# A new order for the first stage of a fused attention and two-layer feed-forward kernel: 128-token pieces of all heads, and two weight loads moved ahead

## The chip, the cores and the metric

The kernel runs on one core of a Trainium2 chip. The metric is the device time of one execution in microseconds (us), the median over the runs. A core has a matrix engine (TensorE, PE in the rows, with PEld for its weight loads), a vector engine (VectorE, DVE), a scalar engine (ScalarE, ACT), a general engine (GpSimd, POOL), and a sync engine (SyncE, SP) that issues most transfers. Each engine works through its own queue in order.

## The reference

Inputs are q, k, v of shape (4 batches, 8 heads, 576 tokens, 64), and five weight matrices which arrive as 64-bit floats.

```python
q_d, k_d, v_d = means over 4 neighbouring tokens            # 144 rows a head
out_up = repeat(softmax(q_d @ k_d.T / 8) @ v_d, 4)          # long range
s = where(abs(i - j) < 4, q @ k.T / 8, -1e9)                # a band of 7 tokens
out_local = softmax(s) @ v
x = (out_up + out_local) as 2304 tokens x 512
x = (silu(x @ w_gate) * (x @ w_val)) @ w_out                # 512 -> 1536 -> 512
h = x @ w2_in                                               # 512 -> 2048
return (h * clip(h + 3, 0, 6) / 6) @ w2_out                 # 2304 x 512
```

## The kernel before, in words

The 2304 tokens go through the feed-forward layers in five blocks (`BLOCKS`, 512 or 384 tokens). A block is 68 units in a fixed order, each with one 128-wide slice of a weight matrix: pairs of `G` (gate), `V` (value), `O` (out), then `H` and `P` of the second layer. A `G`, `V`, or `H` unit is twelve products of 128x128 by 128x512 (`products`, L390): fp32 is split into a high part and a remainder, and three of the four products are taken. The first four of the twelve pairs need only the high part of x.

In block 0 each unit's weights come from the input as a raw piece of 512 KB (`load_raw`), are decoded by `decode_a` (ScalarE, tile `top`) and `decode_b` (VectorE, tile `w`), and split by `split_hi` (ScalarE) and `split_lo` (VectorE) into tile `wr`. Four raw buffers exist at first, so raw piece n+4 is loaded only after `decode_b` of piece n. From unit 0 on, `prefetch` decodes piece i+5 and i+4 and splits pair i+3 while unit i runs. The decoded weights are written to `kept` for the later blocks.

Before unit 0, `first_batch` does the attention of batch 0 on its own (the later batches' attention lies beside the feed-forward work). This stage is called the front. All its PE, DVE and ACT instructions stand in an order written out by hand, `FRONT`, which fixes each of the three queues (`Ordered` keeps program order). A step's name is its function and its index:

- `T`, `E`, `R`: transpose a piece of q or k on PE, evacuate it to SBUF, and sum over groups of four tokens on DVE.
- `dS dM dE dT dP dO dN` (index: pair of heads, 0 to 3): the long-range attention: scores (PE), maximum (DVE), exponential (ACT), transpose (PE), copy (ACT), times v (PE), normalize into `odN` (DVE).
- `SC M W N PT Pa Pd V` (index: 96-token tile, 0 to 5): the local attention: scores and band (PE), maximum (DVE), exponential (ACT, tile `held`), normalize (DVE), transpose (PE), copies (ACT and DVE, tile `turned`), times v (PE, tile `fO`). `V` also adds the long-range part: matmuls of `odN` with `fours`, which repeats each row four times.
- `Xh`, `Xl` (`Yh`, `Yl` for the columns of block 1): write x as high part (ACT) and remainder (DVE) to tile `xr`.
- `to`, `de`, `hi`, `lo`: `decode_a`, `decode_b`, `split_hi`, `split_lo` of the first raw pieces; `de(i)` also issues the load of raw piece i+4.
- `two`, `sums`: GpSimd gathers token sums of batch 1 by transfers and adds; `two` starts behind `M3`.

In the kernel before a `T` is a pair of heads and half of the tokens (three transposes of 96 tokens), and `dS(c)` needs the pieces of pair c alone, while `SC` needs all pairs. `dS` and `PT` use the PSUM banks `acc2` and `acc3`; `dT`, `dO`, `V` use `pa` and `px`; `SC` uses `acc0`, `acc1` or the two `mm` banks. `fill` issues bf16 matmuls whose result nobody reads; `FILL_T`, `FILL_S`, `FILL_P`, `FILL_END` place 69 of them, and `WARM` puts 14 larger ones at the very start.

The SP queue issues, in this order: 16 loads of q and k by head (L148), four loads of v for the long-range values (`load_vd`, tiles `spread` and `vd`), four raw weight pieces, eight loads of v windows (`load_vw`), and then raw pieces 4, 5, ... as `de` frees buffers. GpSimd builds constants, `pick`, `band` and `fours`, and sums the long-range values (`sum_vd`, L478).

Of the kernel before, what the change touches and what calls it, by code (L numbers as in the profile page):

```python
# [32 lines left out]
WARM = 14  # L33
# [20 lines left out]
Tq01 Tq00 Eq00 Eq01 Rq0 Tk00 Tk01 Ek01 Tq10 Ek00 Rk0 Tq11 Tk11 dS0 Eq10 Ek11 Eq11 Rq1 Tq20 Tk10 Eq20  # L54
Tk20 Tq21 dM0 Ek10 Ek20 Rk1 dE0 Tq31 Eq21 Tq30 Tk21 Tk31 Eq31 Tk30 dS1 Rq2 Eq30 Ek21 Ek31 Ek30 Rq3
SC0 dM1 M0 Rk3 dE1 Rk2 dT0 dP0 W0 SC1 dS3 dM3 dT1 dP1 SC2 M1 dE3 W1 dS2 dT3 N0 dM2 dP3 SC3 dE2 dT2
PT0 M2 to0 N1 M3 two dP2 to1 de0 Pd0 W3 dO0 dO3 dN0 dN3 dO2 N3 dO1 Pa0 W2 dN2 dN1 sums to2 PT1
Pa1 Pd1 SC5 SC4 M5 W5 PT3 V1 M4 N2 Pa3 de1 Xh1 W4 V0 Xh0 Pd3 Xl1 N5 de2 PT2 V3 Pd2 Pa2 Xl0 to3 PT5 Xh3
N4 Pd5 Pa5 Xl3 hi0 de3 V2 Xh2 PT4 Xl2 Pd4 Pa4 hi1 V5 lo0 Xh5 V4 Xl5 lo1 Xh4 Xl4 to4 Yh5 Yl5
# [4 lines left out]
def tile_kernel(  # L64
# [58 lines left out]
    for side in range(2):  # L123
        tmp = sp.tile([P, UMAX * UT], F32, tag="sl", name=f"tmp{side}", bufs=3)
        ih = tmp[:, :H]
        nc.gpsimd.memset(ih, 0.0)
        nc.gpsimd.affine_select(
            out=ih, in_=ih, compare_op=ALU.not_equal, fill=NEG,
            base=-(NSEG - 1) * side, pattern=[[-NSEG, H]], channel_multiplier=1,
        )  # L130
        ind = tmp[:, H:H + 1]
        nc.vector.tensor_reduce(ind, ih, axis=AX.X, op=ALU.add)
        on = consts[:, 28 * side:28 * side + 28].rearrange("p (t w) -> p t w", w=W)
        nc.gpsimd.memset(on, 0.0)
        sgn = 1 if side == 0 else -1
        nc.gpsimd.affine_select(
            out=on, in_=on, compare_op=ALU.is_ge, fill=1.0,
            base=-3 if side == 0 else 6, pattern=[[sgn, 4], [sgn, W]], channel_multiplier=0,
        )
        nc.vector.tensor_scalar(on, on, ind[:, 0:1], None, op0=ALU.mult)  # L140
        ones_last.append(on)
# [4 lines left out]
    def late(eng, dst, src):  # L146

        tc.keep_in_program_order(eng.dma_start(dst, src))  # L148
# [105 lines left out]
    top = []  # L254
    if wide:
        for m in range(2):
            top.append(cp.tile([P, DM], I32, name=f"top{m}"))
            nc.gpsimd.memset(top[m], 0)
# [136 lines left out]
    def first_batch():  # L395
# [4 lines left out]
        GT = 6  # L400
        TT = S // GT
        with tc.tile_pool(name="fp", bufs=1) as fp:
# [15 lines left out]
            for hh in range(2):  # L418
                for w in "qk":
                    qn[w, hh] = fp.tile([TT, GT, H // 2, D], F32, tag="fnat", name=f"fn{w}{hh}", bufs=4)  # L420
            for c in range(NC):
                for w, src in (("q", q), ("k", k)):
                    for h in (2 * c, 2 * c + 1):
                        late(nc.sync, qn[w, c // 2][:, :, h % 4], src[0, h].rearrange("(t j) d -> j t d", j=TT))
# [9 lines left out]
            nc.gpsimd.memset(pick, 0.0)  # L434
            nc.gpsimd.memset(band, 0.0)
# [101 lines left out]
            def T(w, c, th):  # L537
                ps = named(("acc0", "acc1", "mm", "mm")[turn[0] % 4], f"fT{w}{c}{th}")
                turn[0] += 1
                ps_of[w, c, th] = ps  # L540
                fill(ps, FILL_T.get(f"{w}{c}{th}", 0))
                for t in range(3):
                    src = qn[w, c // 2][:, 3 * th + t, c % 2 * 2:c % 2 * 2 + 2]
                    pe.transpose(ps[:, t * TT:(t + 1) * TT], src.rearrange("j h d -> j (h d)"), ident[:TT, :TT])

            def E(w, c, th):
                ps = ps_of.pop((w, c, th))[:, :S // 2]
                to = (qT if w == "q" else kT[:, :, 3:])[:, c, th * S // 2:(th + 1) * S // 2]
                scale = 0.125 if w == "q" else 1.0
                if w == "q" and th:  # L550
# [4 lines left out]
            def R(w, c):  # L555
                to, src = (ds, qT) if w == "q" else (dk, kT[:, :, 3:3 + S])
                vec.tensor_reduce(to[:, c], src[:, c].rearrange("p (j t) -> p j t", t=4), axis=AX.X, op=ALU.add)
# [67 lines left out]
            def SC(i):  # L625
# [3 lines left out]
                for par in range(2):  # L629
                    ps = named(f"acc{par}" if i % 2 == 0 else "mm", f"fS{i}_{par}")  # L630
                    if not par:
                        fill(ps, FILL_S.get(i, 0))
                    pss.append(ps[:QT, :NC * WK].rearrange("p (c w) -> p c w", c=NC))
# [39 lines left out]
            def PT(i):  # L673
                for hh in range(2):
                    ps = bank(f"acc{2 + hh}", f"fPT{i}_{hh}")
                    if not hh:
                        fill(ps, FILL_P[i])
# [10 lines left out]

            def V(i):
                ps_of["v", i] = []  # L690
                for h, tag in enumerate(("pa", "acc0") if i == LAST else (("pa", "px")[i % 2],)):
                    n = NC // 2 if i == LAST else NC
                    cs = range(h * n, h * n + n)
                    ps = bank(tag, f"fO{i}_{h}")[:, :n * QT].rearrange("p (c s) -> p c s", c=n)
                    ps_of["v", i].append((slice(h * n, h * n + n), ps))
                    for c in cs:
                        for par in range(2):
                            pe.matmul(
                                ps[par * D:par * D + D, c - h * n], values_of(i)[:WK, 2 * c + par],
                                turned[:WK, i % 2, 2 * c + par], start=c == cs[0], stop=False,  # L700
                            )
                    for c in cs:
                        pe.matmul(
                            ps[:, c - h * n], odN[:, i // 3, c * P:(c + 1) * P], fours[:, i % 3],
                            start=False, stop=c == cs[-1],
                        )
                if i == LAST:
                    fill(bank("acc1", "fend"), FILL_END)

            def X(i):  # L710
                t0 = i * QT
                for cs, ps in ps_of["v", i]:
                    a = 0
                    while a < QT:
                        bi = max(m for m in range(NB) if starts[m] * UT <= t0 + a)
                        e = min(QT, starts[bi + 1] * UT - t0)
                        yield bi, cs, columns(bi, t0 + a - starts[bi] * UT, e - a), ps[:, :, a:e]
                        a = e

            def Xh(i, first=True):  # L720
                for bi, cs, to, xv in X(i):
                    if first == (bi == 0):
                        act.activation(to[:, cs, 0], xv, AF.Copy)

            def Xl(i, first=True):
                for bi, cs, to, xv in X(i):
                    if first == (bi == 0):
                        vec.tensor_tensor(to[:, cs, 1], xv, to[:, cs, 0].bitcast(F32), op=ALU.subtract)
# [3 lines left out]
            def pairs(t):  # L732
                for w, src in (("q", q), ("k", k)):
                    for half in range(2):
                        if not t:
                            st = fp.tile([TT, GT, H // 2, D], F32, tag="fnat", name=f"two{w}{half}", bufs=4)
                            st = st.rearrange("p a h d -> p (a h d)")[:NJH, :2 * H * D]
                            twos[w, half] = st.rearrange("p (h t d) -> p h t d", h=H, t=2)
# [29 lines left out]
            def lo(i):  # L768
# [5 lines left out]
                "Pa": Pa, "Pd": Pd, "V": V, "Xh": Xh, "Xl": Xl, "sums": sums, "two": two,  # L774
                "Yh": lambda i: Xh(i, False), "Yl": lambda i: Xl(i, False), "to": to, "de": de, "hi": hi, "lo": lo,
            }
            for step in FRONT.split():
                name, *arg = re.match(r"([A-Za-z]+?)([qk]?)(\d*)$", step).groups()
                if name in ("T", "E", "R"):
                    w, at = arg  # L780
                    {"T": T, "E": E, "R": R}[name](w, *map(int, at))
# [482 lines left out]
```

## Time and profile before

| | us |
|---|---|
| runs | 940.01, 940.37, 944.05 (median 940.37) |
| the profiled execution | 942.86 |
| its span, first to last instruction | 941.1 |

| engine | busy us | share of the span |
|---|---|---|
| PE | 931.4 | 99% |
| PE weight loads | 794.9 | 84% |
| DVE | 731.3 | 78% |
| ACT | 503.2 | 53% |
| POOL | 106.8 | 11% |

Times in rows are in us from the span's start. A timeline row is: start, duration, engine, line, operation, out<-in, and in brackets the idle time before it and what ended it. The duration of a merged row runs to the end of its last instruction, so the next row may start before it. L160 is the helper that issues all ordered instructions, so tiles tell them apart. The names of tiles: `fT` (transposes), `fdS`, `fdpd`, `fdT`, `fdpT`, `fdO` (long range), `fS`, `held`, `fPT`, `turned`, `fO` (local).

### The profile page before, as it was taken

What the parts mean: (1) busy time and instruction counts of PE and PEld (TensorE: products, weight loads), DVE (VectorE), ACT (ScalarE), POOL (GpSimd) and SP (SyncE); (2) the same over time, 40 slices, a digit from 0 to 9 for tenths busy, and PEclk for the clock granted to TensorE, in tenths of its full rate; (3) what the DMA queues carried; (4) which work ended last, traced back from release to release, by engine and by line L of the source; (5) the groups of instructions that cost most, each with busy time, mean ns of one, the idle gap of its engine ahead of it and who ended that gap; (6) DMA issues with size and microseconds to landing.
All of it is one profiled execution on the core that took longest, in us unless ns stands there. A gap on an engine that the chain in (4) does not pass through costs nothing.

```text
span 941.1 us, 13177 instructions
## 1 busy us (share of the span) xinstructions
PE 931.4 (99%) x4945; PEld 794.9 (84%) x4945; DVE 731.3 (78%) x1044; ACT 503.2 (53%) x946; POOL 106.8 (11%) x117
## 2 busy tenths in 40 slices
PE   9999999999999999999999999999999999999998
PEld 6887888778899988888887778878888888999997
DVE  6968979998898889998835899994437995445653
ACT  5964667877544677453335754533345445444543
POOL 6430012000254200026300000000000000000000
PEclk9999999999999999999999999999999999999999
DMA  9898999768999722759932223533232224443311
GB/s 212 183 291 297 357 380 319 225 207 307 317 248 246 148 90 90 247 165 223 165 109 90 68 90 140 198 112 111 90 103 99 84 96 118 152 134 123 124 45 34
DMA packets 100217, 160.80 MB, mean 171 GB/s; under 512 B 53409, under 2 KB 57377, under 8 KB 100153
## 3 DMA queue, kind: packets, MB, share of 16 engines
q1 hardware_dynamic: 57704, 131.29, 43.6%
q0 software_dynamic: 37408, 10.71, 10.6%
q10 hardware_dynamic: 5040, 17.96, 4.8%
q8 instruction: 39, 0.64, 0.3%
q14 instruction: 26, 0.20, 0.1%
HBM read 137.31 MB, written 22.54 MB: 170 GB/s over the span
## 4 chain that ended last, share of the span: by engine, by line
PE 86%; DVE 7%; ACT 3%; DMA 2%; issue 1%; ACTq 0%; DVEq 0%
PE pH L390 18%; PE aP L1087 18%; PE aO L1087 15%; PE pV L390 14%; PE pG L390 14%; DVE wr L298 1%; PE fO L160 1%; DMA w<-in_moe_w_gate_dram 1%; DMA w<-in_moe_w_out_dram 1%; DVE pv L920 1%; PE pO L814 1%; PE pS L976 1%; DVE xf L952 1%; PE px L940 1%; PE fPT L160 1%
## 5 line engine op out<-in xcount | busy, mean ns | idle before, releaser
L298 DVE TENSOR_TENSOR wr<-w,wr 128x1024 fp32r<-128x1024 f32 x170 | 207.8, 1222 | 115.0 <-ACT wr L293 114.6
L293 ACT ACTIVATE wr<-w 128x1024 fp32r<-128x1024 f32 x170 | 179.5, 1056 | 120.4 <-issue 43.2
L390 PE MATMUL pH<-x,wr 128*128 128x512 f32 (+1 forms) x960 | 210.9, 371 | 0.0
L1087 PE MATMUL aP<-wr,gH 128*128 128x512 f32 x864 | 209.4, 394 | 0.0
L390 PEld LDWEIGHTS pH<-x,wr 128*128 128x128 f32 x960 | 173.5, 188 | 24.4 <-issue 2.1
L1087 PEld LDWEIGHTS aP<-wr,gH 128*128 128x128 f32 x864 | 159.7, 188 | 33.4 <-issue 1.2
L390 PE MATMUL pV<-xr,wr 128*128 128x512 f32 (+1 forms) x720 | 153.2, 368 | 1.6 <-ACT sl L1048 1.6
L390 PE MATMUL pG<-xr,wr 128*128 128x512 f32 (+1 forms) x720 | 154.3, 369 | 0.5 <-DVE sl L1057 0.5
L1087 PE MATMUL aO<-gV,wr 128*128 128x512 f32 (+1 forms) x720 | 153.2, 368 | 0.4 <-DVE wr L298 0.4
L390 PEld LDWEIGHTS pV<-xr,wr 128*128 128x128 f32 x720 | 130.8, 188 | 18.8 <-ACT sl L1048 1.9
L390 PEld LDWEIGHTS pG<-xr,wr 128*128 128x128 f32 x720 | 130.8, 188 | 18.5 <-DVE sl L1057 1.3
L1087 PEld LDWEIGHTS aO<-gV,wr 128*128 128x128 f32 x720 | 130.8, 188 | 17.5 <-DVE wr L298 0.8
L1060 ACT ACTIVATE h<-pH,consts 128x512 f32<-128x512 f32 (+1 forms) x80 | 51.4, 642 | 49.6 <-PE pH L390 48.9
L1048 ACT ACTIVATE sl<-pG 128x512 f32<-128x512 f32 (+1 forms) x60 | 33.2, 553 | 71.4 <-PE pG L390 71.3
L1062 ACT ACTIVATE gV<-sl 128x512 fp32r<-128x512 f32 (+1 forms) x60 | 35.1, 585 | 63.9 <-DVE sl L1057 63.9
L1062 ACT ACTIVATE gH<-h 128x512 fp32r<-128x512 f32 (+1 forms) x80 | 46.7, 584 | 38.9 <-DVE h L1061 38.7
L1063 DVE TENSOR_TENSOR gH<-h,gH 128x512 fp32r<-128x512 f32 (+1 forms) x80 | 50.6, 632 | 12.5 <-ACT gH L1062 12.5
L883 DVE TENSOR_TENSOR pr<-q,k 128x1792 f32<-128x1792 f32 x27 | 54.5, 2020 | 7.1 <-DMA k<-in_k_dram 6.9
L1061 DVE SCALAR_TENSOR_TENSOR h<-h,pH 128x512 f32<-128x512 f32 (+1 forms) x80 | 50.4, 630 | 10.9 <-ACT h L1060 10.1
L920 DVE TENSOR_TENSOR pv<-sc,v 128x1792 f32<-128x1792 f32 x27 | 54.6, 2020 | 0.4
L886 DVE TENSOR_REDUCE sc<-pr 128x28 f32<-128x1792 f32 x27 | 54.3, 2012 | 0.2
L1057 DVE TENSOR_TENSOR sl<-sl,pV 128x512 f32<-128x512 f32 (+1 forms) x60 | 37.6, 627 | 13.4 <-PE pV L390 13.2
(144 smaller groups left out, 767.8 us busy)
## 6 DMA issues: line engine op xcount, KB each, us to landing
w<-kept SPq DMA_DIRECT2D x136, 512.0 KB
kept<-w ACTq DMA_DIRECT2D x34, 512.0 KB
w<-in_moe_w_out_dram SPq DMA_DIRECT2D x21, 512.0 KB
w<-in_moe_w_gate_dram SPq DMA_DIRECT2D x9, 512.0 KB
w<-in_moe_w_val_dram SPq DMA_DIRECT2D x9, 512.0 KB
w<-in_moe_w_in_dram SPq DMA_DIRECT2D x8, 512.0 KB
out_dram<-os SPq DMA_DIRECT2D x15, 256.0 KB
rawsTrue<-in_moe_w_out_dram SPq DMA_DIRECT2D x7, 512.0 KB
```

Of the source, the lines that this page charges most:

```text
L293: behind(nc.scalar.activation(parts[i][:, 0], w32[i // 2].rearrange("p u e -> p (u e)"), AF.Copy))
L298: behind(nc.vector.tensor_tensor(r[:, 1], s, r[:, 0].bitcast(F32), op=ALU.subtract))
L390: nc.tensor.matmul(ps, r[:, a, c], x[:, c, b_, :ps.shape[1]], start=part is HIGH and a == c == 0, stop=part is LOW and c == NC - 1,)
L883: nc.vector.tensor_tensor(pr, qt[:, a:a + SUB, None, :].to_broadcast([P, SUB, W, D]), win(kt, a, SUB), op=ALU.mult)
L886: nc.vector.tensor_reduce(sc[:, a:a + SUB], pr, axis=AX.X, op=ALU.add)
L920: nc.vector.tensor_tensor(pr, pe[:, a:a + SUB, :, None].to_broadcast([P, SUB, W, D]), win(vt, a, SUB), op=ALU.mult)
L1057: nc.vector.tensor_tensor(h, h, ps, op=ALU.mult)
L1060: nc.scalar.activation(h, ps, AF.Relu, scale=1 / 6, bias=half1[:, 0:1])
L1061: nc.vector.scalar_tensor_tensor(h, h, 1.0, ps, op0=ALU.min, op1=ALU.mult)
L1062: nc.scalar.activation(g[:, 0, :nt], h, AF.Copy)
L1063: nc.vector.tensor_tensor(g[:, 1, :nt], h, g[:, 0, :nt].bitcast(F32), op=ALU.subtract)
L1087: nc.tensor.matmul(ps, **one, start=f_ == 0 and a == b_ == 0, stop=f_ == nf - 1 and b_ == 1,)
```

## The change: what it does

A `T` is now a piece of 128 tokens (the last has 64) of all heads, loaded by one transfer each (ten in place of 16), with four transposes into one bank; `E` moves the whole bank, `R` sums all pairs of heads for these tokens. `FRONT` is written anew. Its first `SC` needs only the first pieces; `dS` of any pair needs all pieces. `V` is cut into `Z` (the `odN` part) and `V` (the local part), and the split of the last `V` over two banks goes. The fills of the four tables go; the order has its own (`F:bank:n`), 39 in all; `WARM` is 8. Raw pieces 0 and 1 are issued between the second and the third load of long-range values. `constants()` moves the masks of the later attention and the `top` clears behind the setup of the front, and `pick` and `band` are cleared by DVE.

```diff
-WARM = 14
+WARM = 8
-LAST = 4
-FILL_END = 5
-FILL_P = (4, 4, 4, 4, 4, 0)
-FILL_T = {"k11": 4, "q20": 3, "k20": 5, "q31": 9, "k31": 7}
-FILL_S = {2: 8, 3: 8}
+ON_VECTOR = ('q0', 'k2')
 FRONT = """
...
+Tq0 Tk0 Eq0 Ek0 Tk1 Ek1 Rk0 SC0 Rq0 Tq1 Eq1 M0 Tk2 SC1 Rk1 W0 Tq2 Ek2 Tk3 Rq1 Tq3 Eq2 Tk4 Rk2 Ek3 Eq3 M1 Ek4 Tq4
+Rq2 Eq4 Rk3 W1 SC2 Rq3 Rk4 Rq4 dS0 F:px:22 dM0 dE0 N1 dS1 dM1 dT0 to0 dP0 SC3 M2 de0 dE1 dO0 dS2 F:px:5 dN0 dM2 W2
+dT1 M3 two dP1 N0 F:acc0:6 dO1 dN1 SC4 dE2 dT2 W3 N2 dP2 dS3 dM3 to1 de1 dO2 SC5 dN2 dE3 M4 N3 to2 dT3 PT0 Pd0 dP3
+dO3 dN3 Pa0 W4 de2 PT1 sums Pd1 Pa1 to3 Z0 M5 V0 PT2 Pd2 Z1 de3 V1 Xh0 Xl0 Pa2 W5 PT3 N4 Z2 V2 Pd3 Pa3 Xh1 Xh2 hi0
+PT4 Xl1 Pd4 Z3 V3 Xl2 Pa4 hi1 Z4 Xh3 V4 Xh4 N5 PT5 Xl3 Pa5 Z5 Pd5 V5 F:acc0:6 Xh5 lo0 Xl5 Xl4 lo1 to4 Yh5 Yl5
 """
...
+            for t in range(NPC):
+                for w, src in (("q", q), ("k", k)) if t == 0 else (("k", k), ("q", q)):
...
+                    late(nc.sync, qn[w, t], src[0, :, a:e].rearrange("h s d -> s h d"))
...
-            nc.gpsimd.memset(pick, 0.0)
-            nc.gpsimd.memset(band, 0.0)
+            nc.vector.memset(pick, 0.0)
+            nc.vector.memset(band, 0.0)
...
             for n in range(4):
                 load_vd(n)
+                if n == 1:
+                    load_raw(0)
+                    load_raw(1)
             for n in range(4):
                 sum_vd(n, nc.gpsimd)
-            for n in range(4):
+            for n in range(2, 4):
                 load_raw(n)
...
+            def T(w, t):
+                a, e = piece_of(t)
+                ps = bank(("acc2", "acc3", "pa", "px")[turn[0] % 4], f"fT{w}{t}").rearrange("p (c s) -> p c s", c=NC)
...
+                for c in range(NC):
+                    src = qn[w, t][:, 2 * c:2 * c + 2].rearrange("s h d -> s (h d)")
+                    pe.transpose(ps[:, c, :e - a], src, ident[:e - a, :e - a])
...
+            def Z(i):
+                ps = bank(("pa", "px")[i % 2], f"fO{i}")[:, :NC * QT].rearrange("p (c s) -> p c s", c=NC)
+                ps_of["v", i] = ps
+                for c in range(NC):
+                    pe.matmul(
+                        ps[:, c], odN[:, i // 3, c * P:(c + 1) * P], fours[:, i % 3], start=c == 0, stop=False,
+                    )
```

## Rows read from the trace of the kernel before

**Rows 1.** Busy time in four stretches: five engines, granted clock, DMA share, GB/s

```profile
0.00:53.55 53.55, 51.36 (x572) 41.41 (x572) 42.87 (x91) 37.62 (x153) 28.82 (x55) 1.00 1.01 209
53.55:110.00 56.45, 54.37 (x249) 43.95 (x247) 47.97 (x53) 33.50 (x51) 4.92 (x3) 1.00 0.92 305
...
320.00:941.00 621.00, 615.91 (x3053) 527.93 (x3051) 452.63 (x640) 296.65 (x513) 30.93 (x25) 1.00 0.40 119
```

**Rows 2.** Waits of PE after 53 us: total, times, longest

```profile
PE pV L390 <- ACT sl L1048: 1.6, 1, 1.6
PE pG L390 <- DVE sl L1057: 0.5, 2, 0.3
```

**Rows 3.** Timeline of PE in the front

```profile
1.26 6.16 PE L114 MATMUL warm<-idle 128*128 128x512 bf16 x14 [1.26 <-DVE idle L111]
7.21 0.70 PE L160 MATMUL fTq<-ident,fnq 96*128 96x96 f32 x6
7.75 0.66 PE L160 MATMUL fTk<-ident,fnk 96*128 96x96 f32 x6
...
29.80 4.48 PE L160 MATMUL fdO<-fvd,fdpT 72*72 72x65 f32 x64
34.13 0.60 PE L160 MATMUL fPT<-ident 128*128 128x256 bf16 x4
...
43.60 0.88 PE L160 MATMUL fO<-turned,vw 102*64 102x96 f32 x16
44.41 1.13 PE L160 MATMUL fO<-tmp 72*128 72x96 f32 x8
45.38 0.83 PE L160 MATMUL fPT<-ident,held 96*102 96x96 f32 x8
46.13 0.88 PE L160 MATMUL fO<-turned,vw 102*64 102x96 f32 x16
...
53.55 0.70 PE L390 MATMUL pG<-xr,wr 128*128 128x512 f32 x2
```

**Rows 4.** Timeline of ACT in the front, same columns

```profile
18.22 1.18 ACT L160 ACTIVATE fdpd<-fdS,fdnm 72x144 f32<-72x144 f32 x4 [1.81 <-PE fdT L807]
19.28 0.71 ACT L160 ACTIVATE fdpT<-fdT 72x288 f32<-72x288 f32 x2
19.86 0.36 ACT L160 ACTIVATE held<-fS,fnm 96x102 f32<-96x102 f32 x1
...
22.43 0.74 ACT L160 ACTIVATE fdpT<-fdT 72x288 f32<-72x288 f32 x2
...
28.25 0.92 ACT L266 ACTIVATE top<-w 128x512 f16<-128x512 bf16 x1
28.89 0.82 ACT L160 ACTIVATE fdpT<-fdT 72x288 f32<-72x288 f32 x2
```

**Rows 5.** Groups of DVE work in the front: busy, mean ns, idle before

```profile
L160 DVE TENSOR_REDUCE qdT<-tmp 128x144 f32<-128x576 f32 x4 | 2.9, 748 | 0.3 <-ACT tmp L160 0.2
L160 DVE TENSOR_TENSOR tmp<-fdO,fdsd 72x256 f32<-72x256 f32 x4 | 1.7, 421 | 0.1
L140 DVE TENSOR_SCALAR consts<-consts,tmp 128x28 f32<-128x28 f32 x2 | 1.4, 1298 | 0.0
```

**Rows 6.** Timeline of SP, the transfers' issue

```profile
16.77 19.14 SPq L148 DMA_DIRECT2D vw<-in_v_dram  x8
36.03 6.24 SPq L247 DMA_DIRECT2D w<-in_moe_w_gate_dram  x2
```

**Rows 7.** Transfers of the first 15 us: a queue's packets and MB, one tile's issues

```profile
q1 hardware_dynamic: 9763, 2.65, 106.1%
...
fnq<-in_q_dram SPq DMA_DIRECT2D x8, 144.0 KB
```

**Rows 8.** Busy time in a stretch of 5 us, same columns as rows 1

```profile
15.00:20.00 5.00, 4.49 (x66) 3.74 (x66) 4.15 (x9) 2.50 (x9) 3.10 (x3) 1.00 1.09 235
```

**Rows 9.** A piece of the chain that ended last: start, duration

```profile
64.94 10.56 DMA w<-in_moe_w_gate_dram
```

More of the change, by code (lines that the diff above doesn't have):

```diff
@@ L45 @@
 SUMV = 25
-LAST = 4
-FILL_END = 5
-FILL_P = (4, 4, 4, 4, 4, 0)
-FILL_T = {"k11": 4, "q20": 3, "k20": 5, "q31": 9, "k31": 7}
-FILL_S = {2: 8, 3: 8}
-FRONT = """
[L54 to L59, printed above, removed]
+ON_VECTOR = ('q0', 'k2')
+FRONT = """
+Tq0 Tk0 Eq0 Ek0 Tk1 Ek1 Rk0 SC0 Rq0 Tq1 Eq1 M0 Tk2 SC1 Rk1 W0 Tq2 Ek2 Tk3 Rq1 Tq3 Eq2 Tk4 Rk2 Ek3 Eq3 M1 Ek4 Tq4
[3 more added lines that the diff above has]
+PT4 Xl1 Pd4 Z3 V3 Xl2 Pa4 hi1 Z4 Xh3 V4 Xh4 N5 PT5 Xl3 Pa5 Z5 Pd5 V5 F:acc0:6 Xh5 lo0 Xl5 Xl4 lo1 to4 Yh5 Yl5
 """
@@ L122, in tile_kernel @@
     ones_last = []
[L123 to L141, printed above, removed]
+    top = []
     def flat(ap, off, dims):
@@ L251, in load_unit, with constants @@
             nc.sync.dma_start(w32[i // 2][:, i % 2].rearrange("p (c e) -> p c e", c=2), src)
[L254 to L258, printed above, removed]
+    def constants():
+        for side in range(2):
+            tmp = sp.tile([P, UMAX * UT], F32, tag="sl", name=f"tmp{side}", bufs=3)
+            ih = tmp[:, :H]
+            nc.gpsimd.memset(ih, 0.0)
+            nc.gpsimd.affine_select(
+                out=ih, in_=ih, compare_op=ALU.not_equal, fill=NEG,
+                base=-(NSEG - 1) * side, pattern=[[-NSEG, H]], channel_multiplier=1,
+            )
+            ind = tmp[:, H:H + 1]
+            nc.vector.tensor_reduce(ind, ih, axis=AX.X, op=ALU.add)
+            on = consts[:, 28 * side:28 * side + 28].rearrange("p (t w) -> p t w", w=W)
+            nc.gpsimd.memset(on, 0.0)
+            sgn = 1 if side == 0 else -1
+            nc.gpsimd.affine_select(
+                out=on, in_=on, compare_op=ALU.is_ge, fill=1.0,
+                base=-3 if side == 0 else 6, pattern=[[sgn, 4], [sgn, W]], channel_multiplier=0,
+            )
+            nc.vector.tensor_scalar(on, on, ind[:, 0:1], None, op0=ALU.mult)
+            ones_last.append(on)
+        if wide:
+            for m in range(2):
+                top.append(cp.tile([P, DM], I32, name=f"top{m}"))
+                nc.gpsimd.memset(top[m], 0)
     def halves(ap_, m, dtype):
@@ L687, in Pd @@
                 vec.tensor_copy(turned[:WK, i % 2, 4:], ps_of.pop(("p", i, 1)))
-            def V(i):
[L690 to L702, printed above, removed]
+            def Z(i):
[4 more added lines that the diff above has]
+                        ps[:, c], odN[:, i // 3, c * P:(c + 1) * P], fours[:, i % 3], start=c == 0, stop=False,
+                    )
@@ L703, in V @@
+            def V(i):
+                for c in range(NC):
+                    for par in range(2):
                         pe.matmul(
-                            ps[:, c - h * n], odN[:, i // 3, c * P:(c + 1) * P], fours[:, i % 3],
-                            start=False, stop=c == cs[-1],
-                        )
-                if i == LAST:
-                    fill(bank("acc1", "fend"), FILL_END)
+                            ps_of["v", i][par * D:par * D + D, c], values_of(i)[:WK, 2 * c + par],
+                            turned[:WK, i % 2, 2 * c + par], start=False, stop=c == NC - 1,
+                        )
@@ L710, in X @@
             def X(i):
                 t0 = i * QT
[L712 to L718, printed above, removed]
+                a = 0
+                while a < QT:
+                    bi = max(m for m in range(NB) if starts[m] * UT <= t0 + a)
+                    e = min(QT, starts[bi + 1] * UT - t0)
+                    yield bi, columns(bi, t0 + a - starts[bi] * UT, e - a), ps_of["v", i][:, :, a:e]
+                    a = e
@@ L735, in pairs @@
                         if not t:
-                            st = fp.tile([TT, GT, H // 2, D], F32, tag="fnat", name=f"two{w}{half}", bufs=4)
-                            st = st.rearrange("p a h d -> p (a h d)")[:NJH, :2 * H * D]
+                            st = fp.tile([P, 2, H, D], F32, tag="fnat", name=f"two{w}{half}", bufs=6)
+                            st = st.rearrange("p a h d -> p (a h d)")[:NJH]
                             twos[w, half] = st.rearrange("p (h t d) -> p h t d", h=H, t=2)
```

62 lines of the change are left out of this document (30 added, 32 removed).

## The prediction

> **What bounds the kernel now.** I read the page's first two parts, then the busy time in long stretches, the waits of PE, the timelines of PE, ACT, DVE and SP up to 56 us, and last the transfers. The long stretches [rows 1] show a kernel bound by PE. It stands still for 9.7 of 941.1 us: 2.2 in the front, 2.1 from the first product of the feed-forward layers at 53.55 to 110 us, 0.3 from there to 320, 5.1 behind (some 3 of them at the very end). The only longer single wait behind the front is 1.6 us [rows 2]. So what the change is worth is read at one point: when PE starts its first product, at 53.55 [rows 3]. Behind that point the transfers may be short: from 53.55 to 110 they run at a share of 0.92 [rows 1], and the chain holds a 10.56 us transfer of weights there [rows 9]. That decides whether an earlier first product is kept.
>
> In the front PE looks busy, but 69 fills are in that sum, so I don't take its 51.4 us for need. ACT is the engine to look at in the middle of the front: its rows follow each other without a gap [rows 4]. Towards the end PE runs local values and transposes back to back [rows 3] until the first product.
>
> **Durations.** From one start to the next: on ACT `dE` 1.06, `dP` 0.58, `W` 2.57, `to` 0.64 [rows 4]; on PE a local `V` 0.81, its `odN` part (now `Z`) 0.97, `PT` 0.75, one `dO` a quarter of the 4.33 us between 29.80 and 34.13, so 1.08 [rows 3]. Four fills take 0.60 with their tail; the tail of other matmul rows here is about 0.16, so six fills are 0.65, an estimate. Six transposes of 96 tokens take 0.54 to the next start [rows 3]; four of 128 tokens are by columns 0.48, between 0.36 (no dearer each) and 0.64 (by columns squared). `R` over 576 columns is 0.75 [rows 5]; a piece has 512, so 0.67.
>
> **The start of the front.** Six warm matmuls less save 6 x 0.44 = 2.6 us of PE [rows 3], so transposes may begin at 4.7 in place of 7.2. From then on the transfers pace them. q and k are 16 x 144 KB = 2.36 MB [rows 7]; the queue moved 2.65 MB by 15 us, so the last bytes come at about 13.4 at that rate, and allowing for completion the last piece lands between 13.4 and 15.1; I take 15.1. The new descriptors have the same 256 bytes, so I change no rate. Ten issues replace 16 on SP, which moves what stands behind them forward, not the landing. Once the last piece is there come its transpose, its evacuation and its sums: `W1` starts on ACT at 15.9, the first `dS` on PE at about 17 (it ran at 10.0 before, since one pair of heads was enough). This is what the change pays. What it gets is that `SC0` and `W0` run at 8 to 13 us, before all pieces are there; the old front had its first `W` at 19.86 [rows 4].
>
> **The middle: ACT.** From 15.9 until `dP3` ends, ACT has `W1` to `W3` (7.7), four `dE` (4.2), four `dP` (2.3), `to0` to `to2` (1.9): 16.2 us. Waits that I find by laying the three queues side by side, each step when its engine is free and its input there: 1.5 for `to0` (below), 0.75 where `dP3` waits for `dT3`, which stands behind `SC5` on PE, and some hand-overs, together 2.4. `dP3` ends at 34.5, `dO3` (1.08) and `dN3` (0.42 [rows 5] behind two small instructions, 0.75 in all) end at 36.7.
>
> **The tail: PE.** `Z0` waits for `dN3`, since it needs all heads. From there PE has six `Z` and `V` (10.7), `PT2` to `PT5` (3.0), six fills (0.65): 14.3, with 1.2 of hand-overs: the first product at 52.3. The old order laid out the same way gives 54.1, where the trace has 53.55; so I use the difference, 1.8 us earlier.
>
> **What else moves.** *The fills* that go (69 to 39) and come cost PE, but without any fill the new layout ends only 0.1 us earlier: they lie in waits. *Raw pieces 0 and 1 ahead of two value loads*: `to0` is now in ACT's queue ahead of `dP0`, `dE1` and `W2`, and all of them wait with it. Before raw piece 0 is complete come q and k, two value loads (0.59 MB) and itself (0.52), 3.47 MB; the queue had moved 2.65 at 15 and 3.8 at 20 us [rows 7, 8], so it is there at 18.6, with completion at 19.5 to 21. I used 21; at 19.5 the front is 0.6 shorter, at 23 it is 2.0 longer, at 1 us for 1. Behind two more value loads it would be there near 22, so the move is worth about 1 us, if the order stays. The late values cost nothing: they are in by about 24, GpSimd sums them in 4 us, and `dO2` comes at 31; at 33 they would cost 2.2. *Later raw pieces* do not come earlier by this: piece 4 was issued at 36.03, directly behind eight window loads whose issue took 19.14 us [rows 6], with the same bytes ahead as before. *Constants*: two 1.3 us instructions and three small ones on DVE [rows 5] move from an idle place into the queue of the front, and the clearing of `pick` and `band` comes to it. DVE stands idle for about 4 us in the layout between 6 and 17, waiting for pieces, which hides them; uncovered they cost 0 to 3. I take 0.3, near the hidden end. *The gather of batch 1* starts behind `M3`, which comes 1 to 3 us earlier in the layout, and so its transfers lie a little further from the weights that follow.
>
> **Sum.** -1.8 + 0.3 = -1.5 us: the first product near 52.0. The executed profile, 942.86 (a span of 941.1 and 1.8 around it), would be 941.4. It lies 2.5 above the median of the runs shown, 940.37; the same difference gives 938.9.
>
> **A rule that speaks against it.** The row: 14 dense matmuls of 512 columns at 0.44 us each are at 1.2 GHz, and the transposes that follow at 7.21, 0.09 each for 96 columns, are at 2.4 [rows 3]; but 6 us of dense work went ahead of them and fills stood between them. The Trainium skill (TensorE: Matmul & The Clock Gate, Part 4: PE-mode transpose) says that a run of transposes does not bring the clock up as other matmuls do. No run here shows it alone; by it the time would be that of the next paragraph.
>
> **Rivals.** *B, the slower side: the clock stays at 1.2 GHz.* Dense warm work ends at 4.7, ahead of the 7.2 at which the old front was at the full level, and pieces then leave PE idle between them. Transposes and scores double: laid out with PE low until 12 us, the first product comes 1.05 later than in my layout, until 14 us 1.5, until 17 us 2.45, until 20 us (the 22 fills double as well) 3.45. So from 14 us on it eats the gain: 941.3 at 17, 942.3 at 20. If the clock falls in the 14.3 us tail, where the four fills ahead of each `PT` are gone, half of the tail at half speed adds 7: 946 to 948. For it: sparse work and fewer fills. Against: scores stand between the transposes, and the old tail kept its level over `PT5` and `V2` from 45.38 to 48 without a fill [rows 3], as over 4.3 us of `dO`. *C: nothing is kept.* The first product comes earlier, but weight pieces 11 to 15 do not, and the 2.1 us stand-still before 110 grows by what the front gave: 940.4. For it: the share of 0.92 and the 10.56 us [rows 1, 9]. Against: the load of piece 8 waits for the decode of piece 4, which `to4` begins at the end of the front in both orders, and so moves with it. *D: more.* The stand-still of 2.1 goes as well, since the gather transfers of batch 1 are out of the way, and raw piece 0 is early (0.6): 938.9 - 2.7 = 936.2. *E: the two raw loads land later than meant* (23): -1.5 + 2.0, 940.9.
>
> **How the numbers follow.** My forecast (-0.5 to -2.4, so 938.0 to 939.9) has 0.50, B 0.22, C 0.17, D 0.08, E 0.03. A difference under 0.5% (4.7 us) can't be told from no change here. Faster than 935.7 needs D and half a microsecond more, which is the error of my layout: 0.06, from D and the near end of the forecast. Slower than 945.1 needs the low clock in the tail: 0.08 of B's 0.22. The rest, 0.86, is the same. The range leaves out about one in ten on each side: 936.4 (D) to 943.2 (B at 20 us, and somewhat beyond).
>
> **What would show it.** Right: first `dS` near 17; `held` from about 10; ACT without gaps from 16 to 34 but for one before `top`; `odN` complete near 37, from there PE back to back; the first `pG` at 51 to 53; waits of PE behind it still about 2 us. Wrong in a step: fills of 256 columns at 0.21 us each behind `dS0` or fO rows at twice 0.81 (B); a first `pG` at 52 with a stand-still of 3.5 (C); a gap of over 2 us before the first `top` (E). The forecast falls altogether if the first `pG` comes before 50 or after 55.

## The result, and the profile after

The changed kernel takes 950.78 us (median; 947.06 to 952.87) where the kernel before took 940.31 beside it (939.99 to 944.05): a ratio of 1.0093 [1.0074, 1.0113]. It is slower by 0.9%; the prediction, no difference that can be measured, at 938.9 us within 936.4 to 943.2, was wrong. The profiled execution took 950.48 us, 7.6 more than the one of before.

For some 38 us the front runs as laid out, some 1.5 us late. At 47.30 PE stops. Busy time of the kernel after in four stretches, columns as in [rows 1]:

```profile
0.00:47.30 47.30, 42.74 (x465) 34.41 (x465) 34.47 (x83) 32.97 (x139) 27.29 (x53) 0.96 1.00 194
47.30:54.56 7.26, 0.01 (x2) 0.03 (x1) 0.70 (x2) 1.22 (x2) 2.96 (x3) 0.74 0.99 200
54.56:63.50 8.94, 8.94 (x61) 7.90 (x62) 4.64 (x8) 3.68 (x8) 0.79 (x1) 0.50 0.60 208
63.50:110.00 46.50, 46.34 (x214) 38.15 (x213) 39.86 (x45) 27.99 (x42) 0.00 (x0) 0.99 0.82 280
```

For 7.26 us PE stands, and DVE and ACT all but stand, while the DMA share is 0.99. Behind the stop the granted clock is 0.50, so 1.2 GHz in place of 2.4, until the first product. Behind that PE hardly stands: 0.16 us, where it was 2.1 before. The timeline of PE after, which answers to [rows 3]:

```profile
18.64 0.80 PE L137 MATMUL fdS<-kdT,qdT 64*72 64x144 f32 x8 [0.73 <-DVE kdT L137]
...
46.43 0.88 PE L137 MATMUL fO<-turned,vw 102*64 102x96 f32 x16
54.56 1.99 PE L137 MATMUL fO<-tmp 72*128 72x96 f32 x8 [7.26 <-DVE xr L137]
56.49 1.55 PE L137 MATMUL fO<-turned,vw 102*64 102x96 f32 x16
...
63.72 2.65 PE L386 MATMUL pG<-xr,wr 128*128 128x512 f32 x9
```

The same rows of `fO` take nearly twice what they took before the stop, and the first `pG` starts at 63.72 in place of 53.55. The waiter is `Z4`, which needs the bank that `Xl2` on DVE reads, and that needs `Xh2` on ACT. ACT after, at that place:

```profile
43.69 0.51 ACT L137 ACTIVATE xr<-fO 128x384 fp32r<-128x384 f32 x1
52.97 0.33 ACTq L277 DMA_DIRECT2D kept<-w  x1
53.34 0.49 ACT L137 ACTIVATE xr<-fO 128x384 fp32r<-128x384 f32 x1 [9.13 <-DMA vw<-in_v_dram]
```

Between `Xh1` and `Xh2` stands no arithmetic, but an instruction of ACT's queue that issues a transfer: the write of the second decoded pair to `kept`. It waits until 52.9. The chain of waits of the kernel after shows for what (start, duration, what):

```profile
30.69 22.20 DMA vw<-in_v_dram
...
52.91 0.02 ACTq L277
...
53.86 0.57 DVE xr L137
```

A window load of v, issued at 30.69, ends 22.20 us later, and the chain names its end as what lets ACT go on. The write doesn't read that window; my reading is that the program counts the completion of both on one semaphore and so holds the write back, which no row shows by itself. The windows are late as a whole, as SP after shows, against [rows 6]:

```profile
17.82 27.74 SPq L125 DMA_DIRECT2D vw<-in_v_dram  x8
45.69 6.06 SPq L224 DMA_DIRECT2D w<-in_moe_w_gate_dram  x2
```

Eight window loads hold SP's queue for 27.74 us (19.14 before), and raw piece 4 goes out at 45.69 (36.03). Two other transfers run beside them: the gather of batch 1, issued by GpSimd, and ACT's first write to `kept`. The gather's start on POOL, before and then after:

```profile
30.36 1.86 POOL L742 DMA_DIRECT2D twoq<-in_q_dram  x2 [0.41 <-PE fPT L160]
```

```profile
29.00 1.87 POOL L739 DMA_DIRECT2D twoq<-in_q_dram  x2 [0.32 <-issue]
```

And the queues from 35 to 45 us (packets, MB, share of the 16 engines), before and then after; q1 is SP's queue, q0 the gather's, q10 ACT's writes:

```profile
q0 software_dynamic: 932, 0.99, 69.2%
q1 hardware_dynamic: 1744, 0.73, 41.4%
```

```profile
q0 software_dynamic: 1651, 1.06, 78.1%
q10 hardware_dynamic: 144, 0.52, 15.8%
q1 hardware_dynamic: 598, 0.15, 12.1%
```

The gather moves about the same; SP's queue falls to a fifth, at the same total (174 and 176 GB/s). Two things are mixed in here. Before, SP's 0.73 MB hold a part of raw piece 4, issued at 36.03. And of the 0.58 MB that SP loses, 0.52 go to ACT's write. So these rows don't tell the gather from the write; a run below does. The Trainium skill (DMA: Bandwidth & Descriptors, Queues, rings and completion order) says that an engine takes turns between the queues that have work, a packet each. The rows agree in so far as a queue of small rows loses beside others. Equal turns they neither show nor exclude (1651 packets of q0 to 598 of q1): on that page a packet is a bundle of descriptors, and what the profile counts as one on q1 has some 250 bytes, one row of the load.

### The profile page after: what moved, and what is told of

Same layout as the page of the kernel before. It is cut to its first block, busy times and chain, and to the rows that moved or that the text cites. A ratio compares the mean times of both kernels' runs of the same rounds, so it can differ in the third digit from the quotient of the medians.

```text
span 948.8 us, 13076 instructions
## 1 busy us (share of the span) xinstructions
PE 931.4 (98%) x4901; PEld 796.4 (84%) x4901; DVE 728.0 (77%) x1045; ACT 503.1 (53%) x941; POOL 104.0 (11%) x115
## 4 chain that ended last, share of the span: by engine, by line
PE 82%; DVE 7%; DMA 5%; SPq 2%; ACT 2%; issue 1%; ACTq 0%; DVEq 0%
PE pH L386 18%; PE aP L1089 18%; PE aO L1089 15%; PE pV L386 14%; PE pG L386 14%; DMA vw<-in_v_dram 2%; SPq L125 2%; DVE wr L294 1%; DMA w<-in_moe_w_out_dram 1%; DMA w<-in_moe_w_gate_dram 1%; DVE pv L922 1%; PE pO L816 1%; DMA k<-in_k_dram 1%; DVE pr L885 1%; PE fO L137 1%
```

## The experiments

Theory: the gather, 1.4 us earlier, and a kept write, now in the same stretch (33.75 in place of 46.03), starve the window loads; ACT's held write, `V4` and the clock follow from that. Rivals: the write's place on ACT alone; the order of SP's queue; the missing fills. Single executions of one kernel spread over up to 11 us here (before: 938.9 to 948.6), so beside a ratio with its interval stands what the profiled execution shows.

### What stops, and what the clock costs

The second write behind the last front step (`kw1` issues it): ACT is free of it.

```
-lo1 to4 Yh5 Yl5
+lo1 to4 kw1 Yh5 Yl5
```

> Only the place of the second write of decoded weights in ACT's queue changes: from between Xh1 and Xh2 to behind the last step of the front. Theory A (that write, waiting for the completion semaphore it shares with a load of v windows, is what holds ACT for 9.1 us and so PE for 7.3): the hold of ACT goes, the first pG comes at 52 to 54 in place of 63.7, the time is 939 to 942. Theory B (the window loads themselves are late, and V4 and V5 would wait for them without the write as well): ACT's hold goes, but PE stands before V4 until about 53, the first pG comes at 56 to 60, the time is 943 to 948.

Ratio 1.0029 [0.9996, 1.0061], profiled 945.43. ACT's hold is gone, and the next wait shows, on the window itself. PE of this run:

```profile
52.01 1.55 PE L139 MATMUL fO<-turned,vw 102*64 102x96 f32 x16 [4.74 <-DMA vw<-in_v_dram]
...
59.24 3.09 PE L393 MATMUL pG<-xr,wr 128*128 128x512 f32 x12
```

So the write made a late window later for PE; it did not make it late, as theory B had it.

68 fills ahead of `Z4`, so that PE does dense work during the stop:

```
-hi1 Z4 Xh3
+hi1 F:acc0:68 Z4 Xh3
```

> 68 fills (7.3 us at the full level) ahead of Z4, where PE stands for 7.3 us in the changed kernel; the stop of ACT stays. This splits the loss into the stop and the clock that falls in it. If the clock is worth 4.6 us (9.2 us of rows at 1.2 GHz between 54.56 and 63.7, half of them): the stop becomes fills, Z4 starts at 54.5 to 55 still, the granted clock stays at 1.00, first pG at about 59, time 945 to 947. If the clock falls all the same, or is worth nothing: 949 to 952.

Ratio 1.0033 [1.0012, 1.0054], profiled 945.65. PE of this run:

```profile
46.48 7.60 PE L137 MATMUL ffill<-ident 128*128 128x256 bf16 x68
54.48 1.10 PE L137 MATMUL fO<-tmp 72*128 72x96 f32 x8 [0.41 <-DVE xr L137]
...
59.50 2.79 PE L386 MATMUL pG<-xr,wr 128*128 128x512 f32 x11
```

`Z4` starts as late as in the kernel after (54.48 against 54.56), and the first product 4.2 us earlier. That is the price of the low clock; the remaining 7.8 to the 51.75 of the next run is the stop, 7.26 of which PE stands.

### What makes the windows late

The gather behind `M5` (its guard reads `nm[5]`), and then both edits together:

```
-dT1 M3 two dP1 ... PT1 sums Pd1 ... Z0 M5 V0
+dT1 M3 dP1 ... PT1 Pd1 ... Z0 M5 two sums V0
```

> The gather of batch 1 starts behind M5 in place of M3, about 10 us later; nothing else. Theory B (the gather starves the window loads between 33 and 50 us): the window loads' issue on SP ends near 36 in place of 45.6, the write finds its semaphore free, ACT's hold shrinks from 9.1 to under 2 us, first pG at 53 to 55, time 939 to 943. If the first write of decoded weights at 33.8 us is what starves them instead: hold of 6 us or more stays, time over 946.

> Both edits of the two runs before. If the front has no other trouble than these two, PE runs on without a stop over 1 us from Z0 to the first pG, which comes at 52 to 54 as it was laid out, and the time is 938.5 to 941. If something else holds it as well, the first pG comes after 55 and the time is over 943.

Ratios 1.0010 [0.9982, 1.0038] and 1.0038 [1.0009, 1.0068]. SP and then PE of the first of the two:

```profile
17.49 17.53 SPq L125 DMA_DIRECT2D vw<-in_v_dram  x8
...
67.60 0.33 SPq L125 DMA_DIRECT2D q<-in_q_dram  x1
```

```profile
50.35 0.88 PE L137 MATMUL fO<-turned,vw 102*64 102x96 f32 x16
...
51.75 5.70 PE L386 MATMUL pG<-xr,wr 128*128 128x512 f32 x24
```

The windows go out in 17.53 us, nothing waits, and PE runs back to back to a first product at 51.75. The layout behind the prediction (52.0) was right to 0.3 us, and the tail keeps 2.4 GHz with its few fills. But the time is not below that of before (944.04 beside 941.70): see the part after this one. In the second run the first product comes at 51.26 and the time is no better (946.48, where 938.5 to 941 was expected).

The old kernel with an earlier gather, the strictest test, since nothing of the change is in it (guard on `nm[2]`):

```
-PT0 M2 to0 N1 M3 two dP2
+PT0 M2 two to0 N1 M3 dP2
```

> The kernel before, with only the gather moved: behind M2 instead of M3, so that it starts near 27.9 us instead of 30.36. Theory (how early the gather starts decides when the window loads land): the last window load lands past 48 us instead of 44.3, local values wait for it on PE or ACT waits at its write, first product later than 55, 943 to 948. Rival (it needs the new order's other transfers too): last landing near 44 to 46, first product within 1 us of 53.55, 939 to 942.

Ratio 1.0067 [1.0033, 1.0101], profiled 949.91. POOL, then SP, then PE of this run:

```profile
27.23 1.86 POOL L742 DMA_DIRECT2D twoq<-in_q_dram  x2 [0.52 <-PE fS L160]
```

```profile
15.97 24.38 SPq L148 DMA_DIRECT2D vw<-in_v_dram  x8
```

```profile
53.32 1.55 PE L160 MATMUL fO<-turned,vw 102*64 102x96 f32 x16 [4.88 <-DMA vw<-in_v_dram]
...
61.42 4.93 PE L390 MATMUL pG<-xr,wr 128*128 128x512 f32 x12
```

A gather 3.1 us earlier, and the kernel before loses as the changed one does: windows late, PE waits for one, rows at nearly double length, first product at 61.42 in place of 53.55. ACT's first write has no part in it: it goes out at 45.28 here, behind the last issue of a window. The kernel before stood at the edge of this.

The first write later (behind `N4`), and the raw pieces back behind all value loads:

```
-PT3 N4 Z2
+PT3 N4 kw0 Z2
```

> The changed kernel with the write of the first decoded pair (issued on ACT at 33.75 us, 46.03 in the kernel before) moved behind N4, near 46 us. It tells the gather from this write as what slows the window loads. Theory (the gather's transfers do it, the write adds little): window loads still issued until past 42 us, last one landed past 48, second write still holds ACT for 5 us or more, first product 59 or later, about 947 to 950. Rival (the early write is what tips it): issue ends near 36 to 38, last landing near 44, no hold on ACT, first product near 53 to 54, about 942.

```
-                if n == 1:
-                    load_raw(0)
-                    load_raw(1)
...
-            for n in range(2, 4):
+            for n in range(4):
```

> The changed kernel with raw pieces 0 and 1 back behind all four value loads: that part of the change undone. Theory (the move is worth about 1 us at to0 and has nothing to do with the loss): top waits 1 to 3 us more on ACT, the window loads as late as in the changed kernel (last past 50 us), 949 to 953. Rival (the move sets off the loss through the order on SP's queue): window loads back to a last landing near 44, 942 or less.

Ratios 1.0025 [0.9998, 1.0052] and 1.0016 [0.9987, 1.0045]; profiled 942.86 and 948.67. Neither expectation of mine held. With the first write later (it went out at 40.70) the windows are still late (24.18 us of issue, PE waits 2.29 for the last), but ACT is not held and the first product comes at 55.06. This run tells the gather from the write: from 35 to 40 us no write runs beside the windows in it. The queues in these 5 us, of the kernel before (SP's alone), the kernel after, and this run:

```profile
q1 hardware_dynamic: 721, 0.18, 23.5%
```

```profile
q0 software_dynamic: 436, 0.58, 74.1%
q10 hardware_dynamic: 82, 0.31, 18.9%
q1 hardware_dynamic: 285, 0.07, 12.2%
```

```profile
q0 software_dynamic: 605, 0.58, 102.8%
q1 hardware_dynamic: 179, 0.04, 8.4%
```

Without the write the windows get no more than with it (0.04 and 0.07 MB, where the kernel before moved 0.18): the gather is enough to starve them. With the raw pieces back six of ten executions lie between 940.0 and 940.8, the others between 943 and 951; the profiled one is of the late kind (24.92 us of issue, first product 61.77), so no trace shows the windows of the other kind. By the medians each of the three edits, of the gather, of the first write, or of the raw pieces, undoes the loss to within the noise; in the profiled executions only the later gather brings the windows in time. So the write and the two raw pieces each push a stretch that the gather has brought to the edge. How much each adds stays open.

### Why windows in time are not enough

The gather at two places between: behind `M4` and behind `dM3`.

```
-dE3 M4 N3
+dE3 M4 two sums N3
```

> The changed kernel with GpSimd's gather of batch 1 behind M4 instead of M3, so that it starts near 35.4 us instead of 29.0 (and nearer than the 40 of the run that put it behind M5). Theory (the window loads are starved by the gather's transfers, and the rest follows from that): the eight window loads are issued over about 18 us, the last lands near 39 to 41, ACT's write of the second decoded pair does not wait, first product of the feed-forward layers at 52 to 53, profiled execution 941 to 944, since some of the early gain goes to a q load of the next batch that comes later than in the kernel before. Rival (a gather anywhere ahead of the window loads' end costs the same): last window load past 45, first product past 55, 946 or more.

```
-dS3 dM3 to1
+dS3 dM3 two to1
```

> The changed kernel with the gather of batch 1 behind dM3, the maximum of the last long-range scores, so that it starts near 33 us: between the 29.0 of the changed kernel and the 35.3 and 40.1 of the runs that were later, 2.7 later than the 30.36 of the kernel before. Theory (two ends pull: window loads want the gather late, the q load of the next batch on SP's queue wants it early): last window load landed near 40 to 44, no hold on ACT, first product 51.5 to 53, q load issued near 65 to 68, profiled execution 940 to 943. Rival (there is no middle: either the windows or the q load lose): first product past 55, or the q load past 69, 944 or more.

Ratios 1.0032 [1.0007, 1.0057] and 1.0054 [1.0039, 1.0069]. The gather starts at 35.32 and 33.47, the windows go out in about 18 us, and the first product starts before 52. But the times are not those expected (profiled 945.35 and 946.58), and in the second run it is the rival that came, with the q load past 69 and over 944. PE gives more than the gain back at one wait. DVE, then SP and one of its waits (in all, times, longest), then PE of the second run:

```profile
76.83 2.02 DVE L885 TENSOR_TENSOR pr<-q,k 128x1792 f32<-128x1792 f32 x1 [9.42 <-DMA k<-in_k_dram]
78.78 1.22 DVE L294 TENSOR_TENSOR wr<-w,wr 128x1024 fp32r<-128x1024 f32 x1
```

```profile
71.84 0.33 SPq L125 DMA_DIRECT2D q<-in_q_dram  x1
```

```profile
SPq L125 <- POOL dnk L752: 2.3, 1, 2.3
```

```profile
80.05 6.89 PE L1089 MATMUL aO<-gV,wr 128*128 128x512 f32 x23 [6.01 <-DVE wr L294]
```

The gather ends when its last sum on POOL does (`dnk`), at 71.8. SP's load of the next batch's q and k takes the memory that the front gives up then, and waits for that sum. DVE stands 9.42 us at the first score of that batch, and the split of the next weights, which PE needs, is queued behind it. Behind its wait of 6.01 PE also runs slower for a while: the granted clock is 0.78 from 80.05 to 87.00, and the 23 products take 6.89 where the run with the gather behind `M5` has 5.51. In the kernel before this wait of DVE is 4.34. How long it gets goes by when the gather ends, not by when it starts: behind `M5` the gather starts last of all, at 40.09, ends at 67.6, and DVE waits 4.53. The ten runs in which the gather starts at 32.8 or later have their first product at 51.1 to 53.1, and none is faster than the kernel before.

Masks out of the start of VectorE's queue (step `cs` behind `Xl1`), the first write later too, and the raw pieces back:

```
-Xl1 Pd4
+Xl1 cs Pd4
```

> The run with the gather behind dM3, and the five small VectorE instructions of the masks moved out of the start of the front to behind Xl1. In the changed kernel they stand at the head of VectorE's queue, which waits 6.59 us for GpSimd there and then is busy without a gap until the first dS. Theory (that wait delays everything in the front): first evacuation on VectorE near 4.5 in place of 9.1, first dS near 17 in place of 18.6, first product 1 to 2 us earlier than in the run without this edit, time 0 to 2 us less. Rival (the pieces' landing paces the start, the wait is hidden, as I had costed it): first dS within 0.4 of 18.6 and the same first product.

> The run before this one, with the write of the first decoded pair also moved behind N4 (near 40 us in place of 33). Theory (the write adds 0.5 MB to the stretch in which the window loads are in flight): last window load 1 to 3 us earlier than without the edit, first product 50 to 51.5, 938 to 941. Rival (with the gather at 33 the windows are through in time, the write costs nothing): the same first product within 0.5, the same time within 1 us.

> The gather behind dM3, the masks late, and raw pieces 0 and 1 back behind all value loads. Theory (the move of the raw pieces is worth about 1 us at to0, as forecast, and the 940.7 that undoing it gave to the changed kernel came from a gather that started later against the window loads): to0 waits 1 to 2 us longer, first product 0.5 to 1.5 later than with the move, time 0 to 2 us more. Rival (the move itself costs, through two value loads that come 4 us later or through the queue): first product the same or earlier, time 1 us or more below the run with the move.

Ratios 1.0035 [1.0002, 1.0069], 1.0042 [1.0027, 1.0056], 1.0041 [1.0016, 1.0066]. The masks' wait was real, and taking it away gained almost nothing. DVE of the kernel after, then of the first of these runs:

```profile
8.30 0.16 DVE L241 TENSOR_REDUCE tmp<-tmp 128x1 f32<-128x8 f32 x1 [6.59 <-POOL tmp L236]
```

```profile
4.95 0.69 DVE L137 TENSOR_SCALAR tmp<-fTq 128x512 f32<-128x512 f32 x1 [3.24 <-PE fTq L137]
```

The first evacuation on DVE comes at 4.95 in place of 9.09, the first `dS` at 17.77 against 18.11 without the edit, the first product at 51.66 against 51.76. PE now stands for a later piece, as I had costed it, and then runs at the low clock (a row of PE, and the stretch behind it with the columns of [rows 1]):

```profile
14.06 0.98 PE L137 MATMUL fTq<-ident,fnq 128*128 128x128 f32 x4 [1.96 <-DMA fnq<-in_q_dram]
```

```profile
14.06:17.70 3.64, 3.64 (x30) 3.15 (x31) 1.70 (x4) 2.34 (x10) 0.89 (x1) 0.53 1.06 255
```

In the kernel after the low stretch lies earlier, 0.51 from 9.90 to 13.30, behind 1.87 us in which PE waits for DVE; the edit moved it and did not remove it.

The first write's place costs nothing once the gather starts at 33 (first product 51.89 with it late). The raw pieces' move: `top` starts at 21.29 with it and at 23.16 without, the first product at 51.66 and 52.60. That is the forecast 1 us, in one execution each.

The profiled execution of the third run is the one that keeps its gain. SP and DVE of it:

```profile
65.83 0.33 SPq L125 DMA_DIRECT2D q<-in_q_dram  x1
```

```profile
71.06 2.02 DVE L889 TENSOR_TENSOR pr<-q,k 128x1792 f32<-128x1792 f32 x1 [1.77 <-DMA k<-in_k_dram]
```

The gather ends at 65.8, DVE waits 1.77, no wait of PE up to 110 us is over 0.8, and the execution takes 940.53, 2.3 less than the profiled one of the kernel before. One other took 940.87, the remaining eight 943.3 to 948.7. So this end of the gather moves from one execution to the next; why is open.

Four runs move the first score two units later; the second and the fourth of them move the load for it on SP as well (`CLOAD`):

```
-CLOAD = (2, 6)
+CLOAD = (4, 6)
...
+            wait = 0 if bi else 2
-            lo_, n_ = (0, NU1 - 1 - (bi == 1)) if ph == 0 else (NU1, NU - NU1 - 6)
+            lo_, n_ = (wait, NU1 - 1 - (bi == 1) - wait) if ph == 0 else (NU1, NU - NU1 - 6)
```

> The run with the gather behind dM3, and the first score of batch 1 on VectorE two units later in the feed-forward layers (the six jobs of that kind in block 0 are spread over units 7 to 34 in place of 5 to 34). Theory (the gather that ends late delays the load of q and k, and VectorE stands at the first score with the decode of weight piece 10 behind it): VectorE's wait for k shrinks from 9.4 to under 3 us, the 6.0 us wait of PE for wr goes, 939 to 942. Rival (the weights behind the q load on SP's queue are late by themselves): PE waits 3 us or more for weights of pieces 11 to 13 instead, 943 or more.

> The gather behind dM3, masks and first write moved, first score two units later, and the load of q and k for it two units later on SP's queue as well (behind raw pieces 11 to 13). Theory: first product near 51.5, no wait of PE over 1 us from there to 110 us, 938 to 940. Rival (the later load delays the score as much as the score was moved): VectorE waits over 4 us for k, 942 or more.

> The kernel before with the first score of batch 1 two units later, nothing else. It waits 4.34 us for k there on VectorE, and PE 1.6 us for a silu. Theory (in the kernel before that wait is nearly covered): 939 to 941, within 1 us of the kernel before. Rival (the edit has a gain of its own that has nothing to do with the front): 938.5 or less; or a price, where the six jobs lie closer together: 942 or more.

> As e14, with raw pieces 0 and 1 back behind all value loads. Theory (the raw pieces' move is worth about 1 us at to0 once the windows are in time either way): first product 0.5 to 1 us later than in e14, time 0 to 1 us more. Rival (the move costs, since the window loads behind it come later): last window load 3 us or more earlier than in e14 and time less by 1 us or more.

These don't test what they were meant to. This score is not pinned by program order, and in the first and third run its product `pr` came out at the same place of DVE's queue, between the decode of pieces 9 and 10. So the first run is nearly a repeat of the gather behind `dM3` (1.0033 [1.0013, 1.0053]), the third of the kernel before (0.9990 [0.9967, 1.0012]). In the second and fourth (1.0030 [1.0008, 1.0053] and 1.0023 [1.0006, 1.0041]) `pr` came one decode later and the load went out behind two more raw pieces, but DVE still waited for it 7.9 and 4.3 us, and in the second PE then waited 3.9 and 2.1 for weights. That the wait at the first score is what gives the gain back rests on the rows above and on the one execution without it; no edit took it away.

The gather out of the front, in the new order and in the old one:

```
+            if i == QKAT:
+                last = [t for key, t in state.items() if key[0] == "g"][-1]
+                for _ in down_sums(1, ["qk"], last[:, 0, :1].bitcast(F32)):
+                    pass
...
-            if m % 2 and (bi or m > 8):
+            if m % 2 and (bi or m > 24):
```

> The changed kernel without the gather of batch 1 in the front: those token sums are made between units 13 and 24 of the feed-forward layers in the way that the kernel makes them for the later batches (four transfers a half that add up, no adds on GpSimd), and batch 1's transposes of them start at unit 25 in place of 9. Theory (the gather was all that took the new front's gain): window loads landed by 39, no hold on ACT, first product 51.3 to 52, q load issued before 62, PE stands for under 1.5 us from there to 110, 936 to 939, and 0.5 to 2 us below the same edit in the kernel before. Rival (weights pace the first units whatever comes when, so that an earlier first product only makes PE wait there): PE waits 2 us or more before 110, same time as the kernel before with the same edit within 0.5.

> The same edit in the kernel before. Theory: window loads landed by 38 in place of 44.3, first product within 0.7 of 53.55, no wait of VectorE for k, 937.5 to 939.5. Rival (the gather later costs as much, against the weights at 130 to 165 us): PE waits there, 941 or more.

Ratios 1.0258 [1.0242, 1.0273] and 1.0275 [1.0256, 1.0294]. Both expectations missed the edit's own price: batch 1's transposes were not pinned either and stood in PE's queue right behind unit 13, where PE waits for the gather. PE of the new order, then of the old:

```profile
52.60 1.63 PE L387 MATMUL pG<-xr,wr 128*128 128x512 f32 x6
...
147.29 0.38 PE L366 MATMUL pqT<-ident,dnq 72*128 72x72 f32 x1 [17.79 <-DMA dnq<-in_q_dram]
```

```profile
53.06 1.18 PE L391 MATMUL pG<-xr,wr 128*128 128x512 f32 x4
...
149.38 0.38 PE L370 MATMUL pqT<-ident,dnq 72*128 72x72 f32 x1 [19.59 <-DMA dnq<-in_q_dram]
```

Since both pay it, the pair compares the two fronts only up to that wait: the first product comes 0.46 us earlier in the new one, and PE reaches the wait at 129.50 against 129.79. The medians lie 1.8 us apart, but what parts them is the end of the wait, 147.29 against 149.38, and the intervals overlap. Where the windows were in time, the first product came at 51.1 to 53.1 in the new order and at 53.0 to 53.6 in the old one. So the new order by itself brings it forward by some 1.3 us on average; that the whole kernel gains by it is not shown. No version here beats the kernel before.

## Why the prediction was wrong

- **The failing step** is the last one of "what else moves": the gather starts behind `M3`, "which comes 1 to 3 us earlier in the layout, and so its transfers lie a little further from the weights that follow". It came 1.4 earlier. I asked what lies behind it and not what was still on its way: eight window loads, whose issue in the old profile runs from 16.77 to 35.91 [rows 6], across the gather's 30.36. That term stood at zero and cost 12.0 us at the first product (63.72 against 51.75 with only the gather moved to behind `M5`), 7.8 of stop and 4.2 of clock. What pushed the same way stood nowhere either: ACT's first write 12.3 us earlier, and window loads that begin 1.05 us later (17.82 against 16.77), where I had what stands behind the ten issues move forward.
- **"With the same bytes ahead as before"** was right for the windows as for raw piece 4, and no help: what counted was what came beside them. I costed late values and late raw pieces (23 us in rival E), and no case had a late window, although `V` reads one.
- **ACT's ledger** held: the first `dS` came 1.6 later than laid out (18.64), and `odN` is complete 1.5 later (38.2 against 36.7), so the middle took what it was to take. The ledger had `to`, `dE`, `dP` and `W` in it, but not the two writes that ACT issues. One of them held ACT for 9.13 us.
- **Constants** (0.3): 0.1 measured. **Raw pieces** (about 1 us at the first product): 0.9 measured, but by their place they also push the windows toward the gather. **The first product** (52.0): 51.75 with the windows in time, and that close by luck: in that execution `odN` is complete 1.1 late (37.8), and the tail behind it took 14.0 where I had 15.6.
- **Rival B** had the price of a low clock in the tail (7 us; it was 4.2) and the wrong cause. The fills that went were not needed: in the run with the gather behind `M5` the tail keeps 2.4 GHz. The clock fell because PE stood still for 7.26 us. The early half of B did come, in part: the clock was 0.81 from 4.65 to 13 us, and the first `dS` was late. What that cost is not shown, since with the masks late the low stretch only moved.
- **Rival C**, nothing is kept, is what the medians of the mended versions show, at another place than I put it: not the weights' transfers, but the q load that waits for the gather's memory. At 0.17 it was rated too low: the 0.92 share and the 10.56 us transfer [rows 1, 9] spoke for it, and the old DVE's 4.34 us wait, which I had not looked up, would have pointed to it.
- The last sign that I had written down, a first `pG` after 55, was the right one: it came at 63.72.

## What to carry to other kernels

When a step moves in time, list the transfers that it issues and every load that is in flight then, in the old profile, before costing anything else; a load whose consumer is near has no slack to lend. A write issued from a compute engine's queue can hold that engine, here for 9.13 us. An earlier start is worth only what the next shared resource lets through: here the gather should start late for the windows and end early for the memory that it frees.

## What the runs showed of the hardware

- The windows, 1.25 MB in rows of 256 bytes, go out in 16.3 to 18.4 us where the gather starts at 32.8 or later or does not run there at all, in 19.1 where it starts at 30.4, in 21.9 at 29.8 (the kernel before with the score moved), and in 24 to 28 at 29.0 or before: all of the difference lies within 4 us of its start.
- The clock after the stop stayed at 0.50 for the whole 8.94 us in which PE was busy; 7.60 us of fills in the stop kept it at 2.4 GHz.
- The granted clock reads 1.00 in the first microseconds, [rows 1], where the lengths say otherwise: the 14 warm-up matmuls of 512 columns take 0.44 us each [rows 3], where 68 fills of 256 columns take 7.60, 0.11 each, so 0.22 for 512. So they ran at 1.2 GHz.
